# Pinning the issue order of three kinds of side work in a packed attention and two-layer expert kernel

## The chip, the cores and the metric

The kernel runs on one core of a Trainium2 chip. The metric is the device time of one execution in microseconds, as the median of the runs. Engines are named as in the profile: PE is TensorE's matmul and PEld its weight load, DVE is VectorE, ACT is ScalarE, POOL is GpSimd, SP is SyncE, which issues transfers; a "q" behind a name is the engine's instruction queue.

## The reference

```python
# attention over 32 packed queries, then back: x is (2304, 512)
x = relu(x @ w_in) ** 2 @ w_out                    # (512 x 2048), (2048 x 512)
logits = x @ w_gate                                # 8 experts
P = exp(logits - logits.max())
for _ in range(8):
    P /= P.sum(1, keepdims=True) + 1e-09
    P /= P.sum(0, keepdims=True) + 1e-09
    P *= N / E
out = 0
for e in range(E):                                 # every token goes through every expert
    h = np.maximum(x @ w1[e], 0.0)                 # w1[e]: 512 x 1024
    out += P[:, e:e + 1] * (h @ w2[e])             # w2[e]: 1024 x 512
```

All matmuls of weight are made of three: each float32 operand is split into a rounded high part and a low rest, and high x high, high x low and low x high are added up.

## The kernel before

The 2304 tokens go in three groups of 2 x 256, 2 x 384 and 2 x 512 columns (`GROUPS`, indices p = 0, 1, 2). Attention and the first pair of layers take the span up to about 425 us. Then come three rounds over the experts' weights, cut into 32 pieces n (four per expert).

Round one (line 826) does group 0. `unit(n, 0)` makes the first layer of piece n by a scheme of seven block products in place of eight (`product`, line 663, 42 matmuls of 256 columns; weights and tokens are added and subtracted blockwise beforehand). After four of the products it calls `hook(n, i, at)`, i = 0 to 3, where `at` is the last matmul of the product just emitted. Between the products it emits the second layer of piece n - 1 (`y_unit`, 24 matmuls). The hook splits weights for the pieces to come (`split_w`: block sums on DVE at L128 to L131, the copy on ACT at L151, the rest on POOL at L152, a store of W1 on SP), and does the side work of the table `extra`: the gate's maximum, spread and exponent in units 1 and 2; `keep_gates` in units 8 to 14; `keep_operand` in units 9 to 15, which forms an operand of group 1 by a subtraction on DVE (L426), a copy on ACT (L405) and a rest on POOL or DVE (L406) and stores it on SP for the third round; and three operands of group 2 in units 22, 24 and 26. From the third hook of unit 2 on it also does one half-step of the gate's balancing (`balance`): `rows_step` (L630 to L635, DVE), or `cols_step` (a matmul of the column sums at L640 and then L642 to L645, DVE). The sixteen half-steps take four units.

Round two does group 2, round three group 1, as 16 batches q of two pieces each. A batch's first layer is `layer1` (7 products for each of its two pieces), its second layer `layer2` (line 1016), again seven block products k, for two halves d; layer two of batch q - 1 is emitted between the products of layer one of batch q. Each step k reads an operand made two steps ahead by `op2` (a subtraction on DVE at L1006 or L1008, a copy on ACT at L1010, a rest on POOL at L1011) and a tile of W2 combinations made four steps ahead by `load_a`; its result is added to the output on DVE (L1043), which frees the PSUM bank (`psx` or `psz`). In round two `load_a` calls `make_a(j)`, j = 7 q + k: additions of raw W2 blocks on DVE (L909 for k = 1, L911 to L913 for k = 2), a copy on ACT (L915), the rest on POOL (L916), a store on SP (L917) for round three, and `fetch`, which issues raw W2 blocks on ACT's queue (L890) into four buffers `rb` and one `rbx`. In round three `load_a` loads the stored tile.

What sets the order: the source emits instructions in one order, but a planner in the build (`schedule_with_timeline_sim=True`) puts each engine's instructions in a line by its own timeline: of those emitted, what it takes to be ready first goes first, if its buffer is free by then. The engines run these lines in order. An order can be forced by an edge: within `with tc.issue_after(ins):` every instruction emitted on the engine of `ins` is placed behind `ins`; it is an edge of order and no wait. Before the change there is one such place, in the hook, and `at.ins` is a matmul, so it holds for PE alone:

```python
        if n > 2 or i == 3:
            with tc.issue_after(at.ins):
                balance()
```

Of the kernel before, what the change touches and what calls it, by code (L numbers as in the profile page):

```python
# [1 line left out]

# [1 line left out]

# [33 lines left out]
def kernel(ctx: ExitStack, tc: tile.TileContext, qT, kT, v, pT,  # L38
                                     win, wout, wg, w1, w2, out):
    nc = tc.nc  # L40

    def open_pool(name, **kw):
        st = ExitStack()
        return st, st.enter_context(tc.tile_pool(name=name, bufs=1, reuse_waits="tile", **kw))
# [90 lines left out]
    def split_w(n=1):  # L135
        for _ in range(n):
            k = state["split"]
            if k >= len(splits):
                return
            state["split"] += 1  # L140
            key, l, i = splits[k]
            part = k % 12 >= 8
            w = wpools[part].tile([128, 2, 512], F32R, tag="w", name="w", bufs=4 if part else 8)
            if loads[l][0] == "f64":
                t = from_f64(raw[l])
            elif key[0] == "w2":
                t = raw[l][:, i * 512:(i + 1) * 512]
            else:
                t = w1_blocks(raw[l], i)
            n = t.shape[1]  # L150
            nc.scalar.activation(w[:, 0, :n], t, AF.Copy)  # L151
            nc.gpsimd.tensor_tensor(w[:, 1, :n], t, w[:, 0, :n].bitcast(F32), op=ALU.subtract)  # L152
            W[key] = w
            if key[0] == "w1":
                there = kept.tile([128, 2, 512], F32R, name=f"kept_w1_{key[1]}_{i}")
                nc.sync.dma_start(there[:, :, :n].bitcast(F32), w[:, :, :n].bitcast(F32))
                KEPT[key[1], i] = there, n
            if k + 1 == len(splits) or splits[k + 1][1] != l:
                load_w()
# [282 lines left out]
    def logits(k, new_bank):  # L442
        ps = new_bank()
        for kd in range(4):
            for x in range(2):
                nc.tensor.matmul(ps[:, :256], wgs[:, kd, :], LG[k, kd][:, x, :],
                                 start=(kd + x == 0), stop=(kd + x == 4))
        lgT = gp.tile([2 * E, 256], F32, tag="lgT", name="lgT", bufs=1)
        (nc.scalar.copy if k < 7 else nc.vector.tensor_copy)(lgT, ps[:2 * E, :256])

        pt = new_bank()[:, :2 * E].rearrange("p (t e) -> p t e", t=2)
        for t in range(2):
            nc.tensor.matmul(pt[:, t, :], lgT[:, t * 128:(t + 1) * 128], both, start=True, stop=True)
        nc.scalar.activation(P[:, 2 * k:2 * k + 2, :], pt, AF.Copy)
# [194 lines left out]
    def balance():  # L649

        n = steps["n"]
        if 0 <= n < 16:
            steps["n"] += 1
            if n % 2 == 0:
                steps["cs"] = rows_step()
            else:
                cols_step(steps["cs"])
# [136 lines left out]
    def load_operand(name):  # L794
# [8 lines left out]
    extra = {  # L803
        (0, 1): lambda: logits(7, ybank),
        (0, 2): lambda: logits(8, ybank),
        (1, 2): gate_max,
        (2, 0): gate_spread,
        (2, 1): gate_exp,
        (2, 2): start_balance,
    }  # L810
# [5 lines left out]

    def hook(n, i, at):
        split_w((2, 2, 1, 1)[i])
        if (n, i) in extra:
            extra[n, i]()  # L820
        if n > 2 or i == 3:
            with tc.issue_after(at.ins):
                balance()

    last = None
    for n in range(NQ):
        unit(n, 0, y_units(last) if last is not None else (), {i: lambda at, n=n, i=i: hook(n, i, at) for i in range(4)})
        last = n
# [67 lines left out]
    def fetch(j):  # L896

        q = j // 7
        for name, k, m, d in FETCH.get(j % 7, ()):
            if q + k // 7 < NB:  # L900
                raws[q + k // 7, name] = w2_block(7 * q + k, m, d)

    def make_a(j):

        q, k = divmod(j, 7)
        w = wpools[2].tile([128, 2, 2, 256], F32R, tag="w", name="wa", bufs=4)
        t = raws.get
        if k == 1:
            nc.vector.tensor_tensor(t((q, 3)), t((q, 2)), t((q, 3)), op=ALU.add)  # L909
        if k == 2:  # L910
            nc.vector.tensor_tensor(t((q, 3)), t((q, 3)), t((q, 1)), op=ALU.subtract)  # L911
            nc.vector.tensor_tensor(t((q, 1)), t((q, 1)), t((q, 2)), op=ALU.subtract)
            nc.vector.tensor_tensor(t((q, 4)), t((q, 4)), t((q, 3)), op=ALU.subtract)  # L913
        src = t((q, (1, 3, 4, 3, 1, 5, 6)[k]))
        nc.scalar.activation(w[:, 0], src, AF.Copy)  # L915
        nc.gpsimd.tensor_tensor(w[:, 1], src, w[:, 0].bitcast(F32), op=ALU.subtract)  # L916
        nc.sync.dma_start(KEPT2[BATCHES[q][1]][:, k].bitcast(F32), w.bitcast(F32))  # L917
        A2[q, k] = w
        fetch(j)

    def load_a(j):

        q, k = divmod(j, 7)
        if q >= 2 * NB:
            return
        if q < NB:
            make_a(j)
            return
        w = wpools[2].tile([128, 2, 2, 256], F32R, tag="w", name="wa", bufs=4)
        nc.sync.dma_start(w.bitcast(F32), KEPT2[BATCHES[q][1]][:, k].bitcast(F32))  # L930
        A2[q, k] = w

    def layer1(entry):
# [10 lines left out]
        def free(i):  # L944
            if entry == 1:
                load_a(i)
            elif entry > 1 and (entry, i) not in KEEP:
                load_w1()
# [67 lines left out]
    def layer2(q):  # L1016
# [8 lines left out]
        for k in range(7):  # L1025
            for d in range(2):
                if k in (1, 5):
                    Z[d] = psm.tile([128, 512], F32, tag=f"y{2 + d}", name="psz", bufs=1)[:, :N]
                ps = (Z if k in (1, 2, 5) else X)[d]
                if d == 0:  # L1030
                    op2(7 * q + k + 2)
                first = k in (0, 1, 5)
                for nn in range(2):
                    for u, v in ((0, 0), (0, 1), (1, 0)):
                        nc.tensor.matmul(ps, A2[q, k][:, u, nn, d * 128:(d + 1) * 128], OPS[7 * q + k][v][:, nn, :],  # L1035
                                         start=(first and nn + u + v == 0), stop=(nn == 1 and u == 1),
                                         skip_group_check=True)
                i, j = INTO[k]
                a = acc[:, 2 * i + d, j * N:(j + 1) * N]
                if q % NB == 0 and k in (0, 1, 2, 6):  # L1040
                    nc.scalar.activation(a, ps, AF.Copy)
                else:
                    nc.vector.tensor_tensor(a, ps, a, op=ALU.add)  # L1043
                if d == 1:
                    load_a(7 * q + k + 4)
                if q % NB == NB - 1:
                    finished(p, k, d)
                yield
# [97 lines left out]
```

## Time and profile before

| | |
|---|---|
| median of 3 runs | 1931.26 us (1928.31 to 1939.61) |
| the profiled execution | 1929.34 us |
| its span in the trace | 1927.1 us |
| PE, PEld busy | 1871.7 us, 1698.7 us |
| DVE, POOL, ACT busy | 1308.3 us, 1037.0 us, 826.5 us |
| DMA moved | 403.55 MB, 209 GB/s on average |

The busy times are of one execution, over the whole span; the stages differ, so a stage is read from a window of the trace. In the windows the numbers behind the length are busy us of PE, PEld, DVE, ACT and POOL, each with its count of instructions, then the mean granted clock of TensorE as a share of full speed, the DMA engines' busy share and GB/s. In a timeline a line is start, duration, engine, source line, operation, output and inputs, shape and count, and in brackets the engine's idle time before it and what ended it. In a list of waits a line is the waiting instruction, what it waited for, us in total, times, longest.

### The profile page before, as it was taken

The page shows a single profiled execution, that of the slowest core. Times are in us where ns is not written, and L with a number is a line of the kernel's source. Part 1 is how long each engine was busy: PE and PEld are TensorE (multiplying, and loading weights), DVE is VectorE, ACT ScalarE, POOL GpSimd, SP SyncE. Part 2 cuts the span into 40 slices and gives each one's busy share as a digit, 9 for nine tenths or more (in the row PEclk, how much of TensorE's full clock was granted, in tenths as well). Part 3 has the DMA queues.
Part 4 walks back from the last instruction along what each step waited for, and adds up shares of the span by engine and source line. Part 5 has one row for each costly group of instructions (what it writes and reads, how often), then busy time and mean ns, then how long its engine had stood idle before and what let it go on. Part 6 is the DMA issues. An engine that isn't in the chain of part 4 may idle for free.

```text
span 1927.1 us, 28559 instructions
## 1 busy us (share of the span) xinstructions
PE 1871.7 (97%) x10244; PEld 1698.7 (88%) x10244; DVE 1308.3 (68%) x2103; ACT 826.5 (43%) x1557; POOL 1037.0 (54%) x655
## 2 busy tenths in 40 slices
PE   8999999998799999999999999999999999999998
PEld 7899999997688999887777778778789999999998
DVE  5767676748865666567686788778785565665665
ACT  6667564644455554443333333333334332223232
POOL 3224230547566766366666777777684444444444
PEclk9999999999899999999999999999999999999999
DMA  7412110208577887666676667776688787877874
GB/s 282 150 34 84 59 55 12 83 23 321 213 246 252 275 281 279 230 209 222 230 229 219 213 226 239 243 246 215 210 287 289 257 267 256 264 259 257 262 252 144
DMA packets 153820, 403.55 MB, mean 209 GB/s; under 512 B 14232, under 2 KB 65360, under 8 KB 153680
## 3 DMA queue, kind: packets, MB, share of 16 engines
q1 hardware_dynamic: 118928, 345.10, 52.4%
q10 hardware_dynamic: 34752, 56.63, 9.6%
q8 instruction: 81, 1.33, 0.3%
q14 instruction: 59, 0.48, 0.1%
HBM read 273.96 MB, written 127.72 MB: 208 GB/s over the span
## 4 chain that ended last, share of the span: by engine, by line
PE 41%; issue 4%; POOL 4%; DMA 3%; DVE 2%; ACT 1%; POOLq 0%; DVEq 0%; ACTq 0%
PE psc L671 20%; PE psx L1035 12%; PE psz L1035 9%; DMA rb<-w 3%; POOL hh L1011 2%; POOL wa L916 2%; DVE hb L1008 1%; ACT hh L1010 1%; DVE acc L1043 0%; DVE hb L941 0%; DVE psc L978 0%; PE pso L1058 0%; DVE rb L909 0%; DVE s L983 0%; ACT s L957 0%
## 5 line engine op out<-in xcount | busy, mean ns | idle before, releaser
L671 PE MATMUL psc<-xc,w 128*128 128x256 f32 (+2 forms) x4032 | 788.8, 337 | 4.2 <-DVE s L752 2.4
L671 PEld LDWEIGHTS psc<-xc,w 128*128 128x128 f32 x4032 | 674.2, 190 | 71.4 <-DVE s L752 2.8
L1011 POOL TENSOR_TENSOR hh<-hb,hh 128x1024 fp32r<-128x1024 f32 (+1 forms) x224 | 490.2, 2194 | 408.6 <-ACT hh L1010 348.3
L1010 ACT ACTIVATE hh<-hb 128x1024 fp32r<-128x1024 f32 (+1 forms) x224 | 213.2, 953 | 416.6 <-DVE hb L1008 160.5
L1035 PE MATMUL psx<-hh,wa 128*128 128x512 f32 (+1 forms) x1536 | 353.6, 363 | 0.9 <-POOL hh L1011 0.9
L1035 PEld LDWEIGHTS psx<-hh,wa 128*128 128x128 f32 x1536 | 279.8, 188 | 31.8 <-POOL hh L1011 1.2
L1035 PE MATMUL psz<-hh,wa 128*128 128x512 f32 (+1 forms) x1152 | 270.2, 368 | 23.2 <-DVE acc L1043 23.2
L1035 PEld LDWEIGHTS psz<-hh,wa 128*128 128x128 f32 x1152 | 211.2, 190 | 50.7 <-DVE acc L1043 28.1
L390 PE MATMUL psy<-h,w 128*128 128x384 f32 (+1 forms) x1200 | 222.3, 330 | 0.3 <-ACT x L396 0.3
L701 PE MATMUL psy<-w,hh 128*128 128x512 f32 x768 | 208.3, 399 | 10.1 <-ACT hh L678 8.1
L152 POOL TENSOR_TENSOR w<-raw,w 128x512 fp32r<-128x512 f32 (+1 forms) x128 | 154.3, 1217 | 112.9 <-ACT w L151 103.6
L390 PEld LDWEIGHTS psy<-h,w 128*128 128x128 f32 x1200 | 200.7, 188 | 0.9 <-ACT x L396 0.5
L1043 DVE TENSOR_TENSOR acc<-psx,acc 128x512 f32<-128x512 f32 (+1 forms) x248 | 152.0, 618 | 66.6 <-PE psx L1035 61.3
L1043 DVE TENSOR_TENSOR acc<-psz,acc 128x512 f32<-128x512 f32 (+1 forms) x184 | 112.8, 617 | 81.7 <-PE psz L1035 81.5
L701 PEld LDWEIGHTS psy<-w,hh 128*128 128x128 f32 x768 | 136.4, 191 | 34.9 <-ACT hh L678 9.6
L916 POOL TENSOR_TENSOR wa<-rb,wa 128x512 fp32r<-128x512 f32 x80 | 134.2, 1688 | 49.1 <-ACT wa L915 25.8
L1008 DVE TENSOR_TENSOR hb<-hb 128x1024 f32<-128x1024 f32 (+1 forms) x96 | 138.8, 1446 | 24.0 <-POOL hh L1011 23.5
L941 DVE SCALAR_TENSOR_TENSOR hb<-psc,gate 128x512 f32<-128x512 f32 (+1 forms) x192 | 118.4, 621 | 37.1 <-PE psc L671 33.6
L371 PE MATMUL psh<-at,g 128*128 128x384 f32 (+2 forms) x768 | 127.7, 305 | 0.0
L371 PEld LDWEIGHTS psh<-at,g 128*128 128x128 f32 x768 | 114.7, 190 | 1.7
L152 POOL TENSOR_TENSOR w<-wt,w 128x512 fp32r<-128x512 f32 x64 | 83.3, 1305 | 39.3 <-ACT w L151 25.1
L152 POOL TENSOR_TENSOR w<-cc,w 128x512 fp32r<-128x512 f32 x32 | 42.0, 1314 | 108.0 <-ACT w L151 72.8
(148 smaller groups left out, 1939.5 us busy)
## 6 DMA issues: line engine op xcount, KB each, us to landing
w<-kept_w SPq DMA_DIRECT2D x184, 512.0 KB, 4.4
kept_w<-wa SPq DMA_DIRECT2D x112, 512.0 KB, 3.5
wa<-kept_w SPq DMA_DIRECT2D x112, 512.0 KB, 4.4
kept_w<-w SPq DMA_DIRECT2D x96, 512.0 KB, 4.4
raw<-w ACTq DMA_DIRECT2D x60, 512.0 KB, 4.4
rb<-w ACTq DMA_DIRECT2D x64, 256.0 KB, 4.6
w<-kept_w SPq DMA_DIRECT2D x61, 256.0 KB, 4.2
raw<-win SPq DMA_DIRECT2D x16, 512.0 KB
```

Source lines behind the costliest of these rows:

```text
L152: nc.gpsimd.tensor_tensor(w[:, 1, :n], t, w[:, 0, :n].bitcast(F32), op=ALU.subtract)
L371: nc.tensor.matmul(ps[:, u - begin:w - begin], gw[:, x, m * 128:(m + 1) * 128], at[:, y, g, u - b * S:w - b * S], start=(i == 0), stop=(i ...
L390: nc.tensor.matmul(ps[:, :n], w[:, x, d * 128:(d + 1) * 128], h[:, y, :], start=(i == 0), stop=(i == 11))
L671: last = nc.tensor.matmul(ps[:, :N], w[:, u, o + k * 128:o + (k + 1) * 128], x[v][:, k, :], start=(start and k + u + v == 0), stop=(k == 1 ...
L701: nc.tensor.matmul(ps, h[:, x, o:o + 128], w[:, y, :], start=(n % 4 + m + x + y == 0), stop=(n % 4 == 3 and m == 1 and x == 1), skip_group ...
L916: nc.gpsimd.tensor_tensor(w[:, 1], src, w[:, 0].bitcast(F32), op=ALU.subtract)
L941: nc.vector.scalar_tensor_tensor(HB[q][m, t][:, nn, :], src, 0.0, GATE[p, g // 4][:, t * N:(t + 1) * N], op0=ALU.max, op1=ALU.mult)
L1008: nc.vector.tensor_tensor(src, src, hb[MINUS[k]], op=ALU.subtract)
L1010: nc.scalar.activation(hi, src, AF.Copy)
L1011: nc.gpsimd.tensor_tensor(lo, src, hi.bitcast(F32), op=ALU.subtract)
L1035: nc.tensor.matmul(ps, A2[q, k][:, u, nn, d * 128:(d + 1) * 128], OPS[7 * q + k][v][:, nn, :], start=(first and nn + u + v == 0), stop=(nn ...
L1043: nc.vector.tensor_tensor(a, ps, a, op=ALU.add)
```

## The change

A context `pinned()` is added. For each engine that has an instruction among the last 400 emitted, it opens `issue_after` on the last instruction emitted on that engine; all that is emitted inside is then placed behind these, each on its own engine. It is put around three things: in the hook, for n > 0, around the side work of `extra` and around the balancing, in place of the edge on PE alone; and in `load_a` around `make_a`, so for round two's W2 tiles with their transfers. `split_w`, the logits of unit 0, the operands formed behind round one and the tiles loaded in round three stay as they were.

```diff
+    @contextmanager
+    def pinned():
+
+        traced = nc.cur_bb.bb.instructions
+        with ExitStack() as st:
+            for engine in {i.engine for i in traced[-400:]}:
+                st.enter_context(tc.issue_after(next(i for i in reversed(traced) if i.engine == engine)))
+            yield
...
     def hook(n, i, at):
         split_w((2, 2, 1, 1)[i])
-        if (n, i) in extra:
-            extra[n, i]()
-        if n > 2 or i == 3:
-            with tc.issue_after(at.ins):
+        if n == 0:
+            extra.get((n, i), lambda: None)()
+            return
+        with pinned():
+            extra.get((n, i), lambda: None)()
+            if n > 2 or i == 3:
                 balance()
...
         if q < NB:
-            make_a(j)
+            with pinned():
+                make_a(j)
             return
```

## Rows read from the trace of the kernel before

**Rows 1.** The page: busy us of each engine, share of the span, instructions.

```profile
PE 1871.7 (97%) x10244; PEld 1698.7 (88%) x10244; DVE 1308.3 (68%) x2103; ACT 826.5 (43%) x1557; POOL 1037.0 (54%) x655
```

**Rows 2.** Five windows: from and to, length, busy us of each engine (instructions), clock, DMA.

```profile
440.00:531.00 91.00, 73.56 (x416) 63.09 (x415) 78.05 (x149) 44.53 (x98) 63.19 (x45) 0.92 0.75 273
550.00:650.00 100.00, 100.00 (x623) 87.44 (x623) 58.85 (x107) 51.77 (x124) 65.38 (x55) 1.00 0.75 259
846.00:882.10 36.10, 33.43 (x147) 26.78 (x145) 25.53 (x29) 15.92 (x24) 27.50 (x15) 1.00 0.72 233
882.10:1365.50 483.40, 462.81 (x2004) 379.66 (x2004) 370.10 (x430) 170.81 (x240) 343.03 (x169) 0.99 0.69 228
1365.50:1400.00 34.50, 34.50 (x140) 28.28 (x141) 26.11 (x32) 10.06 (x14) 21.01 (x11) 0.91 0.54 186
```

**Rows 3.** Timeline at the start of the crowded stretch: three operand splits on ACT.

```profile
439.33 2.31 ACT L405 ACTIVATE xc<-x 128x768 fp32r<-128x768 f32 x3 [0.69 <-issue]
```

**Rows 4.** Timeline of PE: the first gate row of unit 8.

```profile
547.38 0.60 PE L778 MATMUL psy<-ident,P 128*8 128x128 f32 x4
```

**Rows 5.** Timeline, 495 to 500 us: how one long stall of PE comes about.

```profile
495.70 2.34 POOL L406 TENSOR_TENSOR xc<-x,xc 128x1024 fp32r<-128x1024 f32 x1
496.11 2.10 DVE L633 TENSOR_TENSOR P<-P,rs 128x144 f32<-128x144 f32 x1
...
498.57 0.42 DVE L749 TENSOR_TENSOR psc<-psc,s 128x256 f32<-128x256 f32 x1
...
499.46 2.08 PE L701 MATMUL psy<-w,hh 128*128 128x512 f32 x4 [4.29 <-ACT hh L678]
```

**Rows 6.** DVE by line, 440 to 531 us: form, count, busy us, mean ns, idle before.

```profile
L130 DVE TENSOR_TENSOR wt<-raw 128x256 f32<-128x256 f32 x7 | 8.4, 1196 | 0.0
L645 DVE TENSOR_TENSOR P<-P,cr 128x144 f32<-128x144 f32 x7 | 7.1, 1010 | 0.1
...
L633 DVE TENSOR_TENSOR P<-P,rs 128x144 f32<-128x144 f32 x8 | 5.8, 728 | 0.2
...
L642 DVE TENSOR_SCALAR cr<-psy 128x8 f32<-128x8 f32 x8 | 1.3, 162 | 4.1 <-PE psy L640 4.1
```

**Rows 7.** The same view, 550 to 650 us.

```profile
L711 DVE SCALAR_TENSOR_TENSOR acc<-psy,P,acc 128x512 f32<-128x512 f32 x8 | 5.8, 747 | 2.3 <-PE psy L701 2.1
L130 DVE TENSOR_TENSOR wt<-raw 128x256 f32<-128x256 f32 x9 | 4.8, 533 | 0.0
```

**Rows 8.** The gate tile's instructions: count, shortest, median and longest ns, first and last start.

```profile
L633 DVE TENSOR_TENSOR P<-P,rs x8: 307/446/2096, 463.8 to 525.1; 128x144 f32<-128x144 f32 x8
L645 DVE TENSOR_TENSOR P<-P,cr x8: 295/798/2216, 473.8 to 531.4; 128x144 f32<-128x144 f32 x8
```

**Rows 9.** Windows cut by batch in round two's first half: two of twelve.

```profile
1130.40:1168.50 38.10, 38.10 (x168) 31.55 (x169) 30.71 (x37) 14.21 (x20) 26.55 (x14) 1.00 0.66 220
1168.50:1208.80 40.30, 38.37 (x171) 31.44 (x169) 31.01 (x37) 14.09 (x20) 31.02 (x16) 1.00 0.77 247
```

**Rows 10.** Waits, 850 to 1480 us: us in total, times, longest us.

```profile
PE psz L1035 <- DVE acc L1043: 23.2, 10, 3.5
DVE rb L909 <- DMA rb<-w: 38.3, 10, 5.8
ACT hh L1010 <- DVE hb L1008: 63.3, 19, 5.3
```

**Rows 11.** Timeline of one batch with its stall.

```profile
1197.11 2.78 ACTq L890 DMA_DIRECT2D rb<-w  x2
...
1207.11 0.99 DVE L909 TENSOR_TENSOR rb<-rb 128x512 f32<-128x512 f32 x1 [4.92 <-DMA rb<-w]
...
1208.02 0.68 DVE L1043 TENSOR_TENSOR acc<-psz,acc 128x512 f32<-128x512 f32 x1
...
1208.76 1.65 PE L1035 MATMUL psz<-hh,wa 128*128 128x512 f32 x6 [1.93 <-DVE acc L1043]
```

**Rows 12.** The line that issues the raw W2 transfers.

```profile
DMA to landing us min/median/max: 3.8/4.6/8.0
```

More of the change, by code (lines that the diff above doesn't have):

```diff
@@ L1 @@
-from contextlib import ExitStack
+from contextlib import ExitStack, contextmanager
 import numpy as np
```

## The prediction

> **What bounds the kernel now.** I read the page first, then windows over the whole span, then the waits of PE, then the timeline around the stalls. The page says that PE is busy for 97% of the span [rows 1], so the whole kernel has about 55 us of idle PE, and an edit that only reorders work can win no more than that plus what the clock loses behind the stalls. The windows say where it lies. Two stretches are fully fed: from 550 to 650 us PE is busy all the time and does 623 matmuls, or 6.23 per us [rows 2]; and one batch of the first half of round two takes 38.1 us with PE busy throughout [rows 9]. Against these two measures I weigh the stretches that the change touches.
>
> The first is 440 to 531 us, units 1 to 6 of round one, which hold the gate's balancing. It did 416 matmuls in 91 us, at a mean clock of 0.92 between the levels 2.4 and 1.2 GHz [rows 2]. At 6.23 per us these are 66.8 us of work, so 24 us are lost. DVE is busy for 78 of the 91 us. What fills it is work of much later units. The operand splits of line 405 run from 439 us on [rows 3], though they are emitted in units 9 to 15 (and three in 22 to 26), and unit 8 only begins near 547 us [rows 4]. The worst stall shows how it hurts: POOL splits a third-round operand for 2.34 us, beside it the gate's row scaling (L633) takes 2.10 us on DVE, the add that the next H tile needs (L749) stands behind it, and PE is idle for 4.29 us [rows 5].
>
> The second is 846 to 1400 us. Twelve batches between two stall ends take 483.4 us [rows 2] where 12 x 38.1 = 457.2 would do: 26.2 lost. In the window before them 147 matmuls took 36.1 us, 33.3 at the clean rate of 168 in 38.1 [rows 2, 9]: 2.8 lost. In the one behind, PE is busy throughout but the clock is 0.91 [rows 2]: 3.1 lost. Together 32 us. PE's waits name one cause, the add that empties a psz bank (L1043), 10 times, and DVE's own waits name the raw W2 transfer in front of L909, 10 times for 38.3 us [rows 10]. The timeline joins them: L909 stands on DVE ahead of the add of psz, waits 4.92 us for its transfer, the add follows at 1208.02, and PE, waiting for the bank, has lost 1.93 us [rows 11]. In the source L909 belongs behind the adds of k = 4 of its batch; there it was put in front of those of k = 1 and 2, two or three steps of 38.1 / 7 = 5.4 us early.
>
> **The change part by part.** No arithmetic and no byte is added or removed. The pin gives each instruction of a block an edge, on its engine, to the last one traced there; the edge orders issue and is no wait, so the planner may put the instruction later but not ahead. The old rule for the balancing, on PE alone, has the same anchor, the product's last matmul, as the new; what is new for it is DVE, ACT, POOL and SP.
>
> *W2 tiles of round two.* make_a(j) is pinned on five queues: the adds on DVE behind the add of the step just done, the ACT copy behind the copy of the operand of step k + 2, the POOL split behind that operand's split, the store on SP behind the last W1 load or store, the raw fetch on ACT behind the same copy. Most of this is where it was, since a tile's buffer comes free only with that step; what moves is L909 and the fetches. A fetch moved back by up to one step still has two steps, 10.8 us, until L909, and transfers land in 3.8 to 8.0 us [rows 12]; so I cost the later fetch at nothing, and if that cover failed it would cost what it costs now. L909's own 0.99 us [rows 11] now lies behind the k = 4 add. The next step writes banks that were emptied three steps earlier, so nothing on PE waits right behind it; what is late next is layer one's evacuation, with DVE busy for 31 of 38 us. Bounds: all 32 us come back, or L909 still costs its 0.99 us in each of 16 batches and 16 come back. The waits of rows 10 name nothing else on PE, so I sit near the upper end and take 27.
>
> *The later operands.* Ten splits with their subtractions leave 440 to 500 us for units 9 to 15 and 22 to 26, where PE is full and DVE has 41 of 100 us free, ACT 48, POOL 35 [rows 2]. Each DVE op there may meet a POOL op: L130 takes 0.53 us on average in the quiet stretch and 1.20 in the crowded one [rows 6, 7]. One split and one unit of 10.6 us: I take 2 us for all of them; bounds are 0 (all in free time) and ten times 1.2, 12 us. Their SP stores move with them, and nobody waits for those before round three.
>
> *The balancing.* Its nine DVE lines cost 4.0 us per iteration now (L645 1.01 us and L633 0.73 us the largest, L642 0.16 us the smallest, each busy time divided by 8) [rows 6]. Without the operand splits beside them L633 and L645 may come down to 0.31 and 0.30 us [rows 8], so an iteration is 2.6 to 4.0 us, if the others stay. A unit is 66 matmuls, 10.6 us, and holds two iterations; DVE's other work there is 58.9 less 5.8 for L711, which those units lack, or 5.6 us per unit [rows 2, 7]. That makes 10.8 to 13.6 us of DVE per unit of 10.6, so DVE is the bound for four units and 1 to 12 us remain lost. I take 7, a little above the middle, because a DVE line this full never lets the clock recover for long. The pins put these ops behind each product's evacuation instead of in front, so what waits is the next L640 matmul, which the gate's column sums reach a hook later.
>
> *Gate maximum, spread and exponent* move with the same pins: five small instructions in units 1 and 2, whose waits are part of the 24 us.
>
> **The sum.** Round two: 32 lost, 27 back. Round one: 24 lost, 7 and 2 kept, 15 back. Together 42 us off the profiled execution's 1929.3 us (span 1927.1 plus 2.2 around it): 1887.3. That execution lies 1.9 us under the median of the three; I split this and say 1888.
>
> **Rivals.** *DVE takes over in round one.* The balancing stays at its upper end, 12 us, and the ten operands cost their 12 us where they land: round one gives nothing back, and the time is 1929.3 - 27 = 1902, with the 1 us towards the median 1903. For it speaks that DVE's need exceeds the unit in nearly all of its range; against it, that the full stretch has 41% of DVE free. The same is what a shared port would do: L130 at 1.20 instead of 0.53 us beside POOL is a row of that kind. The Trainium skill, SBUF — State Buffer, section "Who interferes with whom", says that a DVE instruction with two SBUF inputs and a GpSimd instruction that reads SBUF exclude each other, the second blocked until the first ends. By that rule every moved subtraction and split carries its collision along to the full units, and the time would be this rival's; the mean of 0.53 us in the quiet stretch shows that most of them escape it.
>
> *The stall moves in round two.* L909 leaves but the three adds L911 to L913 and the pinned copies hold back an evacuation or an operand by as much, about 2 us per batch: only round one's 15 us come back, 1929.3 - 15 = 1914, with the same 1 us 1915. For it speaks the DVE load; against it the batch of 38.1 us, in which the same work ran with no stall [rows 9].
>
> *The pins do little.* They order behind the last traced instruction, and where that itself was put early (the W1 splits are not pinned) the block may follow it up: about 1926. Against it: those splits reuse buffers that the running unit frees, so they can't run ahead by more than a unit.
>
> *Slower.* Place: the end of a batch in round two. The adds L911 to L913 now stand behind the k = 5 add and ahead of the next operand's subtraction (L1008). ACT's operand copy already waits for L1008 3.3 us on average, 63.3 us in 19 times [rows 10]. If the adds lengthen that wait until it eats the two steps of lead, 10.8 us, each further us is lost in every one of 16 batches. It decides at 3.5 us per batch over the forecast's: 1888 + 16 x 3.5 = 1944. Against it: three adds at L909's 0.99 us are 3 us, under the lead.
>
> **How the numbers follow.** Forecast 0.55; DVE takes over 0.18; the stall moves 0.15; pins do little 0.05; slower 0.07. The forecast's own bounds, with all of 24 + 32 us back, go down to 1873; the range runs from 1874 to 1916 and so takes in the first two rivals. 0.5% of 1931 is 9.7 us, about what a measurement of this kernel tells from no change: the first three cases lie under 1921.6, so faster 0.88; same 0.05; slower 0.07.
>
> **What would show it.** L909 with no wait for rb and behind the k = 4 add; twelve batches near 38.1 us each; no L405 of 768 columns before 550 us; 440 to 531 us with over 500 matmuls, DVE still above 80% there. Wrong: PE waiting for wa or hh in round two, or idle PE in units 9 to 15. The prediction fails most easily if DVE, not the order, makes the stalls of the balancing.

## The result, and the profile after

The changed kernel takes 1883.8 us (median of four runs, 1881.92 to 1887.14), and the kernel before, run beside it, 1932.97 us (1928.31 to 1939.61): a ratio of 0.9745, 95% interval 0.9712 to 0.9778. The forecast was 1888, with a range from 1874 to 1916.

The helper adds lines, so numbers move by 9 in the first half of the file and by 11 or 12 in the second: L405, L633, L645 and L701 are now L414, L642, L654 and L710; L909 is L920, the adds L911 to L913 are L922 to L924, L915 is L926, and L1035 and L1043 are L1047 and L1055. In the experiments they move by a few more; the text gives the number where a row needs it.

First the page (busy us of each engine, share of the span, instructions), to be read against [rows 1]: the work is the same, to the instruction, and PE's idle time has gone from 55.4 us to 25.5 (span 1927.1 less 1871.7; 1883.0 less 1857.5).

```profile
span 1883.0 us, 28566 instructions
...
PE 1857.5 (99%) x10244; PEld 1688.3 (90%) x10244; DVE 1320.4 (70%) x2103; ACT 833.8 (44%) x1557; POOL 1059.1 (56%) x655
```

Then three of the windows of [rows 2] (from and to, length, busy us and instructions of PE, PEld, DVE, ACT and POOL, granted clock as a share of 2.4 GHz, DMA share, GB/s):

```profile
440.00:531.00 91.00, 83.05 (x512) 71.45 (x513) 68.31 (x158) 47.56 (x110) 57.27 (x47) 1.00 0.68 240
...
550.00:650.00 100.00, 99.76 (x623) 87.51 (x623) 66.34 (x116) 55.69 (x129) 75.39 (x59) 1.00 0.91 317
...
882.10:1365.50 483.40, 482.14 (x2121) 397.19 (x2120) 403.94 (x458) 184.94 (x253) 376.73 (x178) 1.00 0.71 237
```

The crowded stretch of round one does 512 matmuls where it did 416, and its clock is at 2.4 GHz throughout. The two stretches that took in the ten operand splits (the first lies just ahead, at 546.9 us) lose next to nothing: 550 to 650 us does 623 matmuls as before, 650 to 750 us 627 where it did 630. The twelve batches hold 2121 matmuls in place of 2004, with 1.3 us of idle PE in place of 20.6.

Stage by stage, cut at the first product of round one, the first second-layer product of round two (so the first batch's first layer counts with round one), and the last split of a W2 tile that reads `rb` (us, worked out from those instructions' starts in the trace):

| stage | before | after | difference | forecast |
|---|---|---|---|---|
| ahead of round one | 427.7 | 429.6 | +1.9 | 0 |
| round one | 389.4 | 374.5 | -14.9 | -15 |
| round two, first half | 624.7 | 593.4 | -31.3 | -27 |
| the rest | 485.3 | 485.5 | +0.2 | 0 |

Ahead of round one nothing was edited, and the twelve kernels below lie between 426.8 and 428.2 there: the 1.9 us are this execution's.

The tile of raw W2 (instructions: count, shortest, median and longest ns, first and last start; under that what its engine waited for) and the timeline of one batch show how round two changed; [rows 10, 11] hold the same of before.

```profile
L920 DVE TENSOR_TENSOR rb<-rb x16: 682/1422/2517, 800.2 to 1377.9; 128x512 f32<-128x512 f32 x16
...
DMA to landing us min/median/max: 3.0/4.5/8.0
```

```profile
1186.53 0.69 DVE L1055 TENSOR_TENSOR acc<-psx,acc 128x512 f32<-128x512 f32 x1 [1.80 <-PE psx L1047]
1187.14 2.23 DVE L920 TENSOR_TENSOR rb<-rb 128x512 f32<-128x512 f32 x1
```

The transfers land as late as they did [rows 12], but DVE no longer waits for one: L920 stands directly behind the adds and starts at once. Here it takes 2.23 us, and the bank behind it is not late.

### The profile page after: what moved, and what is told of

It reads as the page before. It is cut to its first block, busy times and chain, and to the rows that moved or that the text cites. A ratio compares the mean times of both kernels' runs of the same rounds, so it can differ in the third digit from the quotient of the medians.

```text
span 1883.0 us, 28566 instructions
## 1 busy us (share of the span) xinstructions
PE 1857.5 (99%) x10244; PEld 1688.3 (90%) x10244; DVE 1320.4 (70%) x2103; ACT 833.8 (44%) x1557; POOL 1059.1 (56%) x655
## 4 chain that ended last, share of the span: by engine, by line
PE 85%; DVE 5%; issue 4%; POOL 3%; ACT 2%; ACTq 0%; DMA 0%; POOLq 0%; DVEq 0%
PE psc L680 31%; PE psx L1047 14%; PE psz L1047 11%; PE psy L399 11%; PE psy L710 8%; PE psh L380 6%; POOL hh L1023 2%; POOL wa L927 1%; PE psh L341 1%; PE pp L247 1%; PE s L281 0%; DVE hh L688 0%; PE psy L455 0%; ACT w L160 0%; DVE hb L953 0%
## 5 line engine op out<-in xcount | busy, mean ns | idle before, releaser
L680 PEld LDWEIGHTS psc<-xc,w 128*128 128x128 f32 x4032 | 667.1, 188 | 66.9 <-DVE hb L953 1.2
L1023 POOL TENSOR_TENSOR hh<-hb,hh 128x1024 fp32r<-128x1024 f32 (+1 forms) x224 | 501.0, 2242 | 364.2 <-ACT hh L1022 269.1
L1047 PE MATMUL psx<-hh,wa 128*128 128x512 f32 (+1 forms) x1536 | 351.9, 363 | 2.1 <-POOL hh L1023 0.9
L1047 PEld LDWEIGHTS psx<-hh,wa 128*128 128x128 f32 x1536 | 278.7, 188 | 34.5 <-ACT s L985 4.0
L1047 PE MATMUL psz<-hh,wa 128*128 128x512 f32 (+1 forms) x1152 | 265.1, 362 | 0.0
L1047 PEld LDWEIGHTS psz<-hh,wa 128*128 128x128 f32 x1152 | 209.1, 188 | 22.5 <-DVE acc L1055 0.3
L710 PE MATMUL psy<-w,hh 128*128 128x512 f32 x768 | 204.6, 396 | 4.7 <-DVE hh L688 3.9
L1055 DVE TENSOR_TENSOR acc<-psx,acc 128x512 f32<-128x512 f32 (+1 forms) x248 | 151.0, 619 | 73.0 <-PE psx L1047 68.8
L1055 DVE TENSOR_TENSOR acc<-psz,acc 128x512 f32<-128x512 f32 (+1 forms) x184 | 113.7, 618 | 89.7 <-PE psz L1047 89.6
L710 PEld LDWEIGHTS psy<-w,hh 128*128 128x128 f32 x768 | 135.5, 189 | 30.0 <-DVE hh L688 5.4
L953 DVE SCALAR_TENSOR_TENSOR hb<-psc,gate 128x512 f32<-128x512 f32 (+1 forms) x192 | 117.9, 621 | 46.6 <-PE psc L680 43.4
L1020 DVE TENSOR_TENSOR hb<-hb 128x1024 f32<-128x1024 f32 (+1 forms) x96 | 134.0, 1396 | 9.8 <-POOL hh L1023 9.4
L926 ACT ACTIVATE wa<-rb 128x512 fp32r<-128x512 f32 x80 | 48.7, 629 | 119.7 <-DVE rb L924 41.3
```

Source lines behind the costliest of these rows:

```text
L680: last = nc.tensor.matmul(ps[:, :N], w[:, u, o + k * 128:o + (k + 1) * 128], x[v][:, k, :], start=(start and k + u + v == 0), stop=(k == 1 ...
L710: nc.tensor.matmul(ps, h[:, x, o:o + 128], w[:, y, :], start=(n % 4 + m + x + y == 0), stop=(n % 4 == 3 and m == 1 and x == 1), skip_group ...
L953: nc.vector.scalar_tensor_tensor(HB[q][m, t][:, nn, :], src, 0.0, GATE[p, g // 4][:, t * N:(t + 1) * N], op0=ALU.max, op1=ALU.mult)
L1020: nc.vector.tensor_tensor(src, src, hb[MINUS[k]], op=ALU.subtract)
L1023: nc.gpsimd.tensor_tensor(lo, src, hi.bitcast(F32), op=ALU.subtract)
```

## The experiments

**My theory:** each half of the gain has its own cause. In round two it is the place of one DVE instruction, L909, ahead of the adds that empty PE's banks; in round one it is the ten later operands, which crowd DVE beside the balancing. What stays lost in round one is DVE's load per unit. **The rivals:** the ACT, POOL and SP side of the W2 block (its fetches above all) does it in round two; the balancing's own pins do it in round one; a part gains only together with the other.

In these kernels the helper takes two optional arguments: `without` leaves engines out, `only` names those that get an edge.

### Round two: one instruction, the whole block, the block without DVE

`x1_l909` is the kernel before with one edge: L909 alone, on DVE.

```diff
         if k == 1:
-            nc.vector.tensor_tensor(t((q, 3)), t((q, 2)), t((q, 3)), op=ALU.add)
+            with pinned(only=(nc.vector.engine,)):
+                nc.vector.tensor_tensor(t((q, 3)), t((q, 2)), t((q, 3)), op=ALU.add)
```

> The kernel before with one pin only: the addition L909, one instruction in each of 16 batches, on DVE behind the last instruction emitted there. Theory one (the early place of L909 makes the stalls of round two): nearly all of round two's 31.5 us come back, so about 1902 against some 1933, and no wait of L909 for its transfer. Rival (the tile chain as a whole must be in order, fetches and copies included): under 10 us come back, 1923 to 1933.

`x2_w2` is the kernel before with the change's W2 part alone; `x3_w2_no_dve` is the same without DVE's edges.

```diff
-            make_a(j)
+            with pinned():
+                make_a(j)
```

> The kernel before with all of the W2 tiles' work pinned and the hook as it was. Both theories: round two's 31.5 us alone, about 1902 (1898 to 1906), and round one as before (389 us from its first to its last matmul). If the two parts of the change help each other, it is above 1908.

```diff
-            make_a(j)
+            with pinned(without=(nc.vector.engine,)):
+                make_a(j)
```

> The kernel before with the W2 tiles' work pinned on ACT, POOL and SP but not on DVE, so that the additions L909 to L913 may go early. Theory one: L909 still waits for its transfer and the stalls stay, 1923 to 1936. Rival: most of the gain is here, about 1902 to 1910.

On one chip, against 1938.5 us before: x1 1893.53 (ratio 0.9771, 0.9736 to 0.9806), x2 1897.51 (0.9789, 0.9753 to 0.9825), x3 1929.77 (0.9949, 0.9919 to 0.9979). By stage, round two's first half takes 624.7 us before, 589.1 in x1, 593.4 in x2 and 626.4 in x3; round one is at 389.4, 389.4, 389.3 and 391.0. The windows of the twelve batches, x1 first, then x2:

```profile
882.10:1365.50 483.40, 483.40 (x2135) 400.46 (x2134) 402.29 (x457) 179.04 (x251) 370.69 (x178) 1.00 0.74 240
```

```profile
882.10:1365.50 483.40, 482.31 (x2122) 397.83 (x2121) 399.36 (x452) 182.84 (x249) 374.47 (x176) 1.00 0.72 240
```

In x3 the waits of DVE and of PE from 795 to 1480 us (total us, times, longest) are those of before, only more of them; over the same stretch L909 waited 42.9 us in 11 times before, and PE as in [rows 10]:

```profile
DVE rb L920 <- DMA rb<-w: 51.6, 13, 5.0
```

```profile
PE psz L1047 <- DVE acc L1055: 25.4, 13, 2.8
```

So sixteen edges, one per batch on one engine, give everything that round two has to give: with them PE is never idle in these 483 us. The rival of the fetches falls: with the block's edges on ACT, POOL and SP and none on DVE the stall stays. And the rest of the block's pins cost 4.3 us (593.4 against 589.1); where, the last group of experiments shows.

### Round one: the hook alone, and its halves

`x4_hook` has the changed hook and leaves make_a as it was; `x5_operands` pins only the later operands, `x6_balance` only the balancing.

```diff
-        if (n, i) in extra:
-            extra[n, i]()
-        if n > 2 or i == 3:
-            with tc.issue_after(at.ins):
+        if n == 0:
+            extra.get((n, i), lambda: None)()
+            return
+        with pinned():
+            extra.get((n, i), lambda: None)()
+            if n > 2 or i == 3:
                 balance()
```

> The kernel before with the pins of the hook alone (later operands, gate, balancing), W2 tiles as they were. If the parts add up: round one's 15 us, about 1918 (1914 to 1922), with round two's ten stalls still there. If the rest of the schedule shifts with them, it is off by more than 5 us.

```diff
         if (n, i) in extra:
-            extra[n, i]()
+            if i == 3:
+                with pinned():
+                    extra[n, i]()
+            else:
+                extra[n, i]()
```

> The kernel before with pins around the later operands alone (units 9 to 15 and 22 to 26), gate and balancing as they were. Theory (their splits crowd the balancing): most of round one's 15 us, 10 to 15, so 1918 to 1923 against some 1933. Rival (the place of the balancing's own DVE work behind the evacuations counts): under 5 us, 1928 or more.

```diff
         if n > 2 or i == 3:
-            with tc.issue_after(at.ins):
+            with pinned():
                 balance()
```

> The kernel before with pins around the balancing's half-steps alone, on all engines; the operands are free to go early. Theory (the operands crowd): 0 to 5 us of gain, 1928 to 1933, with the splits still at 440 to 500 us. Rival (order of the balancing): 10 to 15 us, 1918 to 1923.

x4 1930.79 (0.9956, 0.9929 to 0.9983, on the chip of x1); x5 1926.39 (0.9941, 0.9921 to 0.9962) and x6 1941.61 (1.0025, 1.0006 to 1.0044), both against 1938.1 on another chip. x4 and x5 lie above the 1914 to 1922 and 1918 to 1923 that I expected, which started from some 1933. By stage, round one gains 9.9 us in x4 and 14.7 in x5, and takes 1.5 us longer in x6. The crowded window of x5, and of x6:

```profile
440.00:531.00 91.00, 83.46 (x506) 72.53 (x505) 72.28 (x161) 46.82 (x109) 56.66 (x47) 0.98 0.71 255
```

```profile
440.00:531.00 91.00, 70.95 (x416) 60.50 (x415) 75.07 (x149) 44.29 (x97) 62.63 (x45) 0.96 0.75 272
```

With the operands held back alone, 506 matmuls, and round one at 374.7 us, the changed kernel's 374.5. With the balancing held back alone, 416, as before, and 390.9 us; the operand splits are still there:

```profile
438.96 2.31 ACT L416 ACTIVATE xc<-x 128x768 fp32r<-128x768 f32 x3 [0.69 <-issue]
```

The rival of the balancing's pins falls. What x4 lacks of round one's gain is for the most part L909 again (L922 there). The first one stands at the end of round one, ahead of the rest of an H tile that PE reads next, and PE is idle for 1.87 us. From 750 to 780 us x4 does 165 matmuls at a clock of 0.94, where x10 below, with the same hook and L909 pinned, does 187 at 1.00:

```profile
771.02 0.69 DVE L922 TENSOR_TENSOR rb<-rb 128x512 f32<-128x512 f32 x1 [5.37 <-DMA rb<-w]
771.63 0.75 DVE L690 SCALAR_TENSOR_TENSOR hh<-psc,hh 128x256 fp32r<-128x256 f32 x2
772.10 0.73 PE L712 MATMUL psy<-w,hh 128*128 128x512 f32 x2 [1.87 <-DVE hh L690]
```

Round two has its stalls as before. PE's waits from 795 to 1480 us:

```profile
PE psz L1048 <- DVE acc L1056: 31.4, 14, 3.5
```

Before, this wait was 23.2 us in 10 times [rows 10], and round two's first half takes 11.2 us longer in x4, and 5.3 in x5, than the 624.7 before. That does not show that round two took back a part of the gain: those 624.7 us are of a short execution, in a kernel whose times differ by 20 us. By the medians x4 is 7.7 and x5 11.7 us faster than before, and the intervals of the ratios, 3.3 to 13.8 and 7.4 to 15.3 us, hold the 9.9 and the 14.7.

### What stays lost in round one

`x7_short_balance` is the changed kernel with one balancing iteration in place of eight; `x8_pace` spreads the eight over more units, three steps per unit in place of four.

```diff
-        if 0 <= n < 16:
+        if 0 <= n < 2:
```

> The changed kernel with one iteration of the balancing in place of eight (seven are left out of the computation). Theory (what is left of round one's loss, 9 us, is DVE's time for the balancing): 7 to 10 us under the changed kernel, about 1875, and no idle PE between 460 and 520 us. Rival (what is left comes from the weights' splits in the same units): within 3 us of the changed kernel.

```diff
-            if n > 2 or i == 3:
+            if (n > 2 and i != 2) or i == 3:
                 balance()
```

> The changed kernel with the balancing left out of the third hook of each unit (where the block sums of W1 stand), so three half-steps to a unit and the end in unit 7 in place of 6. If DVE's load per unit is what is left: 2.6 to 3.5 us less of it in each unit, 10.8 us or less per 10.6, so 3 to 8 us under the changed kernel, 1876 to 1881. Rival (the chain of the half-steps itself stalls PE, whatever the load): as the changed kernel, 1884, with the same waits of L649.

x7 1874.13 (0.9682, 0.9663 to 0.9701), x8 1883.35 (0.9727, 0.9708 to 0.9746), both on the chip of x5. Round one: 374.5 us in the changed kernel, 365.7 in x7, 376.0 in x8. The window of x7, then of x8:

```profile
440.00:531.00 91.00, 88.17 (x553) 77.74 (x552) 59.66 (x112) 51.35 (x122) 62.64 (x52) 1.00 0.80 280
```

```profile
440.00:531.00 91.00, 83.24 (x506) 72.31 (x505) 73.82 (x157) 48.72 (x112) 57.02 (x48) 0.98 0.70 244
```

PE's waits from 430 to 800 us, of the changed kernel, of x7 and of x8:

```profile
PE psy L710 <- DVE hh L688: 3.9, 4, 1.4
PE psy L649 <- DVE cs L644: 2.2, 3, 0.7
```

```profile
PE psy L710 <- DVE hh L688: 1.4, 1, 1.4
```

```profile
PE psy L710 <- ACT hh L687: 2.5, 4, 1.2
PE psy L649 <- DVE cs L644: 2.3, 2, 1.3
PE psy L710 <- DVE hh L688: 1.4, 1, 1.4
```

Seven iterations cost 8.8 us, so the rival in my expectation, the weights' splits, falls. In the window 440 to 531 us, 5.1 of them are idle PE (7.95 against 2.83), and the column sums' matmuls (L649) are another 2.3, since PE is busy 2.7 us with 16 of them against 0.4 with two; 1.4 us are not accounted for. The lines of PE in that window, of the changed kernel and of x7 (count, busy us, mean ns, idle before):

```profile
L649 PE MATMUL psy<-cs,ones 128*128 128x8 f32 x16 | 2.7, 240 | 2.2 <-DVE cs L644 2.2
```

```profile
L649 PE MATMUL psy<-cs,ones 128*128 128x8 f32 x2 | 0.4, 264 | 0.0
```

In x8, PE's waits are as long, 8.2 us in all against 7.9, in part at other instructions, and the 3 to 8 us that I expected did not come. It does not follow that DVE's load is not the cause, for x8 did not lower it. These are the 60 us of the balancing, of the changed kernel and of x8, where the eighth iteration ends a little later:

```profile
460.00:520.00 60.00, 53.45 (x328) 45.98 (x327) 52.25 (x129) 29.96 (x67) 36.47 (x29) 1.00 0.72 254
```

```profile
460.00:520.00 60.00, 55.17 (x329) 48.09 (x330) 52.80 (x120) 29.34 (x67) 36.53 (x30) 0.97 0.74 250
```

DVE is busy for as long while PE does as many matmuls: a unit of x8 has fewer steps, but other operations last longer in it (the rest of an H tile from SBUF, L688, 1.24 us on average in place of 0.83, from 440 to 531 us). What is shown is that the balancing makes the loss, some 0.7 us of idle PE per iteration. Whether DVE's load makes it, or the chain of a step, which goes from DVE to PE and back, stays open.

### The two that matter, and what the other pins cost

`x9_l909_operands` puts x1 and x5 together: one edge for L909, and the later operands pinned. `x10_l909_hook` is x1 with the changed hook, so it has the changed kernel's pins except those on the rest of make_a.

> The kernel before with two pins only: L909 on DVE, and the later operands; gate, balancing and the rest of the W2 tiles' work as before. If the parts add up by stage: round one 374.7 us as with the operands alone, round two 589.1 us as with L909 alone, 1927.1 - 14.7 - 35.6 = 1876.8 of span, some 1878.5 in all, 4 to 7 under the changed kernel's 1884. Rival (the balancing's pins are needed once the operands are gone from beside it): 1883 or more.

> The changed kernel's hook, and of the W2 tiles' work only L909 pinned. Theory (the pins on the rest of that work cost PE half a us in about every second batch): 4 us under the changed kernel, 1879 to 1881, no wait of PE's weight load for line 985's copy. Rival (the balancing's pins count in the presence of the operands'): equal to the kernel with L909 and operands within 1 us if they do not, at least 3 us below it if they do.

`x11_act_free` is the changed kernel without ACT's edges in make_a; `x12_adds_free` is the changed kernel without DVE's edges in make_a, except L909's.

```diff
-            with pinned():
+            with pinned(without=(nc.scalar.engine,)):
                 make_a(j)
```

> The changed kernel with the W2 tiles' work not pinned on ACT (copies and raw fetches free), else as it is. Theory (the pinned copy stands ahead of the copies of layer one and waits on ACT for L913's addition): the seven waits for line 985's copy go, round two 589 to 591 us in place of 593.4, 1880. Rival (it is the additions on DVE that hold things up): 593 as it was.

```diff
         if k == 1:
-            nc.vector.tensor_tensor(t((q, 3)), t((q, 2)), t((q, 3)), op=ALU.add)
+            with pinned(only=(nc.vector.engine,)):
+                nc.vector.tensor_tensor(t((q, 3)), t((q, 2)), t((q, 3)), op=ALU.add)
...
-            with pinned():
+            with pinned(without=(nc.vector.engine,)):
                 make_a(j)
```

> The changed kernel with L911 to L913 not pinned on DVE; L909 and the work on ACT, POOL and SP stay pinned. Rival to the kernel with ACT free: the additions pinned behind the k = 5 add make the copy wait; then round two is 589 to 591 us here, 1880. If the copy's pin alone does it: 593 as it was.

On one chip, against 1940.23 us before:

| kernel | median us | ratio (95%) | round one | round two, first half |
|---|---|---|---|---|
| x9 | 1878.74 | 0.9694 (0.9673 to 0.9714) | 374.5 | 589.1 |
| x10 | 1879.33 | 0.9696 (0.9675 to 0.9717) | 375.6 | 589.2 |
| x11 | 1878.99 | 0.9694 (0.9669 to 0.9719) | 375.9 | 590.3 |
| x12 | 1880.45 | 0.9705 (0.9683 to 0.9726) | 375.8 | 589.8 |

x9 holds the best of both halves, with fewer edges than the change, and the parts add up: I expected a span of 1876.8 us from the stages of x1 and x5, and it is 1876.2. Its four runs (1878.29 to 1879.09) lie 5 us below the changed kernel's four (1881.92 to 1887.14). The two were not run side by side, but the stages say where the 5 us are: in round two's 593.4 against 589.1. x10 and x9 differ by 0.6 us, so pinning the balancing is worth nothing here either.

With the 4.3 us goes this wait of PE's weight loads in the changed kernel, from 795 to 1400 us, and one in front of it on ACT:

```profile
PEld psx L1047 <- ACT s L985: 4.0, 7, 0.8
```

```profile
ACT wa L926 <- DVE rb L924: 41.3, 16, 4.6
```

ACT's copy of a W2 tile waits for the last of its three adds, 2.6 us in each batch, and layer one's evacuation (L985) is queued behind it on ACT. In x10, where neither is pinned, the same wait is 4.9 us in all, and no weight load waits for L985:

```profile
ACT wa L929 <- DVE rb L927: 4.9, 15, 1.6
```

In x11 it is this one, and the twelve batches are full again; the 1.2 us by which x11 is still behind x1 go with a single wait for another evacuation (L953) near 821 us, 1.2 us of PE's weight load, which the changed kernel has too and x12 has not:

```profile
ACT wa L928 <- DVE rb L926: 19.8, 16, 4.6
```

```profile
882.10:1365.50 483.40, 483.40 (x2135) 400.27 (x2134) 402.63 (x457) 180.73 (x254) 369.18 (x179) 1.00 0.73 239
```

x12 has 2135 matmuls there too, though this wait is 65.1 us in it: with the adds free ACT still waits, but not ahead of an evacuation that PE needs soon. Freeing either side is enough, so it takes both pins together to make the loss. Adds and POOL's splits collide as well, two of the adds taking 1.9 and 1.8 us in the median of the changed kernel, where both took 0.68 before. But in x12 two of them take 2.3 us, and its batches are full: longer adds alone are not the cause, and the order on ACT, which x11 changed, is what is left. The tile of raw W2 in the changed kernel and in x12:

```profile
L923 DVE TENSOR_TENSOR rb<-rb x16: 674/1858/2796, 815.6 to 1387.1; 128x512 f32<-128x512 f32 x16
L924 DVE TENSOR_TENSOR rb<-rb x16: 678/1776/2884, 818.3 to 1387.7; 128x512 f32<-128x512 f32 x16
```

```profile
L925 DVE TENSOR_TENSOR rb<-rb x16: 693/2290/2306, 807.3 to 1380.4; 128x512 f32<-128x512 f32 x16
L926 DVE TENSOR_TENSOR rb<-rb x16: 677/2283/2290, 808.0 to 1383.3; 128x512 f32<-128x512 f32 x16
```

## Why the prediction was right, point by point

**Round two: 27 of 32 us.** The cause, L909's place, was right, and x1 shows it with that one instruction. 31.3 us came back. Three sizes were off. What could come back was not 32 us but 35.6 (x1). The short term is the twelve batches: I took them at 12 x 38.1 us and found 26.2 lost, but the window held 2004 matmuls, and at the 168 per 38.1 us of [rows 9] these are 454.5 us, so 28.9 lost; by x1's rate, 2135 in 483.4 us, it is 29.7. Counting matmuls, as I did for the other two windows, would have been better. And L909's own time, for which I kept 5 us, costs PE nothing behind the adds: in x1 PE has no wait on it. What is lost instead, 4.3 us, is the other pins of make_a, which I had put at nothing. That these two errors cancel is luck.

**Round one: 15 of 24 us.** 14.9 came back. The rate of 6.23 matmuls per us, carried to the crowded stretch, held: 512 matmuls are 82.2 us of the 91, so 8.8 are still lost, where I kept 7 and 2. x7 shows that the balancing is what holds them, and it takes 3.5 us of DVE per iteration (its nine lines, 28.0 us for eight), inside my 2.6 to 4.0. But the steps from there to 7 us are not borne out. DVE is not full for four units: from 460 to 520 us it is busy for 52.25 of 60 us while PE is idle for 6.55, and for 68.3 of the 91 us, 75%, in the window for which I had named "above 80%". The clock, which I did not expect to recover, is at 1.00. Of the 7.9 us that PE waits from 430 to 800 us, 6.3 end at a DVE instruction, so the loss passes through DVE; whether DVE's load makes it, x8 leaves open. My sum was wrong as well: 4.0 us less 0.71 and 0.42 for L645 and L633 are 2.9, not 2.6, and by the same steps at least 3 us remain lost, not 1 (and 1.01 us for L645 is its mean over the seven that the window holds, not its busy time divided by 8). The wide bound saved the term, and that 7 in it came out near was luck.

One row of the crowded stretch I misread too: the split of 1024 columns in [rows 5] is an operand of group 2, so of round two and not of the third round. The argument about it does not depend on that.

**The later operands: 2 us, bounds 0 to 12.** They cost next to nothing that a row shows: from 550 to 750 us, 1250 matmuls where it did 1253, half a us. The collisions came along (a subtraction of 2.00 us is shown below), but DVE has the room. So what I had put down to them is the balancing's.

**The rivals.** "DVE takes over in round one" asked for no gain there, and round one gained 14.9. "The stall moves in round two" had the mechanism: the pinned copies and the three adds do hold back an evacuation, and PE's weight loads wait for it. I had priced it at all of round two's gain; it is 4.3 us. "Slower" named the adds and a wait on ACT as well, but asked for 3.5 us per batch, and 4.3 us over 16 batches are 0.3. "The pins do little" did not come about either: the blocks stay in their units, the first operand split at 546.9 us. The rule of the Trainium skill behind the first rival holds, as the section on the hardware shows; the price that the rival put on it does not follow, because in the full units the longer operations are hidden.

**The signs I named.** L920 has no wait for rb: so it is. Over 500 matmuls from 440 to 531: 512. No operand split of 768 columns before 550 us: the first is at 546.9, since unit 8 now begins near 534 instead of 547 [rows 4]; it is in its unit, and the date was what I should have left out. Twelve batches near 38.1 us: 1.3 us of idle PE in all of them. PE waiting for wa or hh in round two, which would have shown me wrong: neither appears among PE's waits there; idle PE in units 9 to 15 is 0.24 us from 550 to 650.

**The median.** x1 gains 45 us by the medians of its call, and 35.3 by the profiled spans (1927.1 and 1891.8). The difference is the kernel before: the execution that I worked from was one of its short ones, as the section on the hardware shows. I had added 1 us for that.

## What to carry to other kernels

Look at what stands in front of the instruction that PE waits for, on that instruction's own queue: one add that waits for a transfer, placed two or three steps early, cost 36 us in 16 batches. Pin that instruction, and the block that crowds the busiest engine, and measure the two alone before pinning whole blocks on every engine: the further edges here brought nothing, and two kinds of them together cost 4 us. While a wait on a transfer makes the time scatter, judge a gain elsewhere by its stage or by medians of many runs, not by the total of one execution.

## What the runs showed of the hardware

**A wait on a transfer makes the time vary.** Kernels in which L909 waits scatter from run to run, those without it far less: the kernel before took from 1929.56 to 1950.77 us in 19 runs on one chip, x4 from 1918.46 to 1935.86, x6 from 1936.93 to 1949.20; in four runs each, x1 took from 1893.21 to 1894.26, x9 from 1878.29 to 1879.09, the changed kernel from 1881.92 to 1887.14. The kernel before and x1 differ in the place of L909 alone. The stall is the rest of a transfer's time at the moment when DVE gets there, and within one execution landing varies from 3.8 to 8.0 us [rows 12]; that it varies between runs in the same way was not measured.

**A small DVE operation can last until POOL's split is done.** In the changed kernel the balancing's L653, a multiplication of 128x8 numbers, takes from 0.17 to 1.21 us. The timeline shows what sets it: the one that overlaps no split on POOL takes 0.17 us, and each of the other seven ends 0.02 or 0.03 us behind the split that it overlaps. Here one starts while POOL splits W1, and ends with the split (478.04 and 478.06); L651 in front of it, which reads PSUM, takes its 0.16 us under the same split. Below them a moved operand's subtraction lasts until 601.95, 0.81 us past the end of the POOL split at 601.14; where no split overlaps it, such a subtraction takes 0.95 us (at 612.43).

```profile
476.75 1.29 POOL L161 TENSOR_TENSOR w<-wt,w 128x512 fp32r<-128x512 f32 x1 [0.78 <-POOL w L161]
476.76 0.16 DVE L651 TENSOR_SCALAR cr<-psy 128x8 f32<-128x8 f32 x1
477.19 0.87 DVE L653 TENSOR_SCALAR cr<-cr 128x8 f32<-128x8 f32 x1
...
599.84 1.30 POOL L161 TENSOR_TENSOR w<-raw,w 128x512 fp32r<-128x512 f32 x1 [0.43 <-ACT w L160]
599.95 2.00 DVE L435 TENSOR_TENSOR x<-x 128x768 f32<-128x768 f32 x1
```

The operations of the same tiles, by count and shortest, median and longest ns:

```profile
L653 DVE TENSOR_SCALAR cr<-cr x8: 171/832/1210, 471.2 to 516.4; 128x8 f32<-128x8 f32 x8
L651 DVE TENSOR_SCALAR cr<-psy x8: 156/158/167, 470.5 to 515.9; 128x8 f32<-128x8 f32 x8
L644 DVE TENSOR_REDUCE cs<-P x8: 412/438/447, 468.8 to 514.0; 128x8 f32<-128x144 f32 x8
```

The one that reads SBUF stretches fivefold, from its shortest to its median; the one from PSUM (L651) stays as it is, and the reduction (L644) nearly so: 0.41 or 0.42 us beside no split, 0.43 to 0.45 under one. The Trainium skill, SBUF — State Buffer, section "Who interferes with whom", has this rule: a tensor_tensor with both inputs in SBUF, or a tensor_scalar in a mode that takes both ports, and a GpSimd operation that reads SBUF wait for each other to end, while on trn2 a reduction never does. This trace agrees on each: L435, L653 and L644. What it costs here is little: in the full units such an operation is hidden, and in the balancing it is a part of the 5.1 us of idle PE, how large a part was not measured.
